# Gate and up units in four PSUM banks, four units written where the value weights were, and the last tile's column pieces one after the other

## The chip, the cores and the metric

The kernel runs on one core of one Trainium2 chip. The metric is the device time of one execution in microseconds (us). Before the change it is 226.32 us, the median of 3 runs (226.05 to 226.35).

## The reference, cut to what matters

For 2048 tokens of 512 features, with LayerNorm output xn shared by two branches:

```
xn  = layernorm(x)
q, k, v = heads(xn @ wqkv)                     # 32 heads of 16
phi(a)  = [softmax(a @ w_phi), softmax(-a @ w_phi)]
kv, z   = sum over tokens of phi(k) v^T, sum over tokens of phi(k)
A   = (phi(q) kv) / (phi(q) z + 1e-6) @ wo     # linear attention: kv needs all tokens
B   = ((xn @ w_gate) * (xn @ w_up)) @ w_down   # 1792 hidden features
out = x + A + B
```

All inputs and the output are bfloat16.

## The kernel before, in words

Tokens go in 16 tiles of 128 (index t) and in 4 groups of 512 (index g). The hidden features of branch B go in 14 blocks of 128 (index ft). The work falls into these pieces; each is a Python function that records steps for the engines:

- `ln`/`emit_xn` (lines 410 to 445): LayerNorm of a tile on VectorE, and its transpose, by TensorE for t below 8 and by a transposing DMA on SyncE's queue for the rest.
- `wprime(w)`: folds `w_phi` into the key weights (w=1) or the query weights (w=0); four steps of four small matmuls, each copied out by ScalarE.
- `k_pe(t)`: values of a tile, 4 matmuls of 512 columns that read the value weights `wv`, copied out by ScalarE. `k_pe(12)` to `k_pe(15)` are the last readers of `wv`.
- `k_pk(t)` and `k_norm(t)`: the keys' softmax. `emit_exp` (line 463) has ScalarE copy the 512 columns twice (plain and negated), VectorE take a maximum by a tree (L476) and subtract it (L482), and ScalarE take the exponential. `emit_sums` (L496) is a tree of additions on VectorE; `k_norm` then takes a reciprocal (L520) and multiplies (L523).
- `emit_kv(half)`: the sum over 8 token tiles, 64 matmuls of 65 columns for each half. `emit_kv(1)` needs `k_norm(15)`, the last of the keys, and `q_pk` writes banks that it uses.
- `q_pk(t)`, `q_scale(t)`, `q_T(t)`, `q_num(t)`, `q_oT(t)`: the queries' softmax by the same trees, a transposing DMA of 128x1024 on SyncE's queue, 8 matmuls of 68 columns into banks 3 and 4, a division on VectorE (L614, L615), and a second transposing DMA.
- `glu(g, ft)`, a unit: 4 matmuls of 512 columns for the gate and 4 for the up projection, each into a PSUM bank of its own. ScalarE copies the gate bank to SBUF (L277, the line of every ScalarE step), and VectorE multiplies it with the up bank (L545) into the hidden buffer `hT`.
- `final(t)`: 18 matmuls for a tile's output (14 blocks of `w_down`, 4 of `wo`), in three steps of 7, 7 and 4; VectorE adds x (L642) and SyncE's queue stores the tile. The last tile is cut into columns 0 to 383 and 384 to 511, which lie in banks 7 and 5.

All matmuls are issued by one helper at L297.

PSUM has 8 banks. Up to the queries, `next_a` (line 430) hands out banks 0 to 4 in turn for transposes, `k_pe`, `k_pk`, `wprime` and `emit_kv`. The units rotate through banks 5, 6 and 7 while g is below 3: one unit has 5 and 6, the next 7 and 5, the next 6 and 7. Units of g=3 alternate gate in 5 and up in 6; in the queries' stage banks 0 to 2 belong to `q_pk`, 3 and 4 to `q_num`, and 7, 5, 6 to `final`.

The hidden buffer of g=2 and 3, `hTb`, lies where the normalized keys `ek` lie, so units of g=2 with their place in `hTb` and all of g=3 are bound to when `ek` has been read: those of g=2 go over the keys of tiles 0 to 6, which `emit_kv(0)` has read, those of g=3 over the keys of tiles 7 to 13, most of which `emit_kv(1)` reads.

The order of the steps on each engine is set at build time. A list scheduler, `_order` (line 714), walks through all steps with estimated costs; an engine takes the step that can start first by the estimate, and of those that can start the one of lowest priority number. Steps count in the order they are written; units have priorities from 1e6, `final` from 2e6, so they fill what the others leave. Copies and multiplies of the units have -1 and the output additions -2. On the chip each engine then runs its own steps strictly in that order and waits with semaphores, and SyncE's queue issues its DMAs in order as well. So a change of a bank or of a place changes which steps depend on which, and through the estimate the order on all engines.

Of the kernel before, what the change touches and what calls it, by code (L numbers as in the profile page):

```python
# [197 lines left out]
def _build(nc, es, A_x, A_wqkv, A_w_phi, A_wo, B_w_gate, B_w_up, B_w_down, out):  # L198
# [59 lines left out]
    def sbv(name, lo, n):  # L258
        off = layout[name] + lo
        return arena[:, off:off + n]  # L260
# [5 lines left out]
    def bank(b, lo=0, n=512):  # L266
        return psum[:, b * 512 + lo: b * 512 + lo + n]
# [4 lines left out]
    def act_op(out_ap, in_ap, func=ACTF.Copy, scale=1.0, bias=None, prio=None):  # L272
        def fn(e):
            kw = {}
            if bias is not None:
                kw["bias"] = bias
            return e.activation(out=out_ap, in_=in_ap, func=func, scale=scale, **kw)  # L277
        r = [in_ap]
        if isinstance(scale, bass.AP):
            r.append(scale)  # L280
        if isinstance(bias, bass.AP):
            r.append(bias)
        return sc.step(ACT, fn, reads=r, writes=[out_ap], cost=(50.0 if str(in_ap.tensor.name) == "ps" else 95.0) + 0.833 * in_ap.free_size(),
                       lat=180.0, prio=prio)

    def dve(fn, reads, writes, n, rate=1.0, fixed=65.0, prio=None):
        return sc.step(DVE, fn, reads=reads, writes=writes, cost=fixed + rate * n / 0.96, lat=150.0, prio=prio)
# [4 lines left out]
    def mms(items, prio=None, warm=False):  # L292

        def fn(e):
            ins = None
            for o, l, r, a, z in items:
                ins = e.matmul(o, lhsT=l, rhs=r, start=a, stop=z)  # L297
            return ins
        reads = []
        writes = []  # L300
        c = 0.0
        for o, l, r, a, z in items:
            reads += [l, r]
            writes.append(o)
            c += max(25.0, o.free_size() / 2.4 + 2.3) * (1.6 if warm else 1.0)
        return sc.step(PE, fn, reads=reads, writes=writes, cost=c, lat=260.0, prio=prio)

    def group(o, pairs):
        n = len(pairs)
        return [(o, l, r, i == 0, i == n - 1) for i, (l, r) in enumerate(pairs)]  # L310
# [8 lines left out]
    def x_tile(t):  # L319
        return sbv("x", t * 512, 512)  # L320
# [3 lines left out]
    def xnT(q, s_lo, n):  # L324
        return sbv("xnT", q * S_TOK + s_lo, n)
# [17 lines left out]
    def load_wT(w, at):  # L343

        return sc.dma(SP, wT_v[:, w, :, :], A_wqkv[:, w * 512:(w + 1) * 512], transpose=True, at=at, issue=4600.0)
# [80 lines left out]
        return sbv("xn", (t % 4) * 512, 512)  # L426

    a_bank = [0]

    def next_a():  # L430
        b = a_bank[0] % 5
        a_bank[0] += 1
        return b

# [15 lines left out]
    def wprime(w):  # L450
        for dt in range(NQ):
            b = next_a()
            mms([(bank(b, jt * 128, 128), wT_v[:, w, jt, dt * 128:(dt + 1) * 128], wbd_v[:, jt, :], True, True)
                 for jt in range(NQ)])
            act_op(Wp_v[:, w, dt, :], bank(b))
# [50 lines left out]
    def k_pe(t):  # L506
        b = next_a()
        mms(group(bank(b), [(xnT(q, t * 128, 128), wv_v[:, q, :]) for q in range(NQ)]))
        act_op(vext_all[:, t, :, 0:64], bank(b).rearrange("p (c j) -> p c j", c=8))

    def k_pk(t):
        b = next_a()
        mms(group(bank(b), [(xnT(q, t * 128, 128), Wp_v[:, 1, q, :]) for q in range(NQ)]))
        p_slot["k", t] = emit_exp(b, ek_v[:, t, :])

    def k_norm(t):
        slot = t % 3
        sm = emit_sums(ek_v[:, t, :], p_slot["k", t], slot)
        rs = rs_v[:, slot, :]
        dve(lambda e: e.reciprocal(out=rs, in_=sm), [sm], [rs], 64, rate=6.0)  # L520
        e4 = ek_v[:, t, :].rearrange("p (g f h) -> p g f h", g=16, f=16)
        r4 = rs.rearrange("p (g h) -> p g h", g=16)
        dve(lambda e: e.tensor_tensor(out=e4, in0=e4, in1=r4[:, :, None, :].to_broadcast([128, 16, 16, 4]),  # L523
                                      op=ALU.mult), [ek_v[:, t, :], rs], [ek_v[:, t, :]], 1024, rate=0.5)


    def hT(g, ft, lo, n):
        return sbv("hTa" if g < 2 else "hTb", ((g % 2) * NF + ft) * 512 + lo, n)

    glu_ctr = [0]  # L530

    def glu(g, ft, banks):
        i = glu_ctr[0]
        glu_ctr[0] += 1
        bg = banks[(2 * i) % len(banks)]
        bu = banks[(2 * i + 1) % len(banks)]
        gr = sbv("gring", (i % 3) * 512, 512)
        base = 1e6 + i * 10
        mms(group(bank(bg), [(wg_v[:, q, ft * 128:(ft + 1) * 128], xnT(q, g * 512, 512)) for q in range(NQ)]),
            prio=base)  # L540
        mms(group(bank(bu), [(wu_v[:, q, ft * 128:(ft + 1) * 128], xnT(q, g * 512, 512)) for q in range(NQ)]),
            prio=base + 1)
        act_op(gr, bank(bg), prio=-1.0)
        dst = hT(g, ft, 0, 512)
        dve(lambda e: e.tensor_tensor(out=dst, in0=bank(bu), in1=gr, op=ALU.mult), [bank(bu), gr], [dst], 512,  # L545
            prio=-1.0)
# [5 lines left out]
    def emit_kv(half):  # L552
        for g in range(8):
            b = next_a()
            mms(group(bank(b, 0, 65), [(ek_v[:, t, g * 128:(g + 1) * 128], vext_all[:, t, g, 0:65])
                                       for t in range(half * 8, half * 8 + 8)]))
            kp = kvp_v[:, g, :]
            if half == 0:
                act_op(kp, bank(b, 0, 65))
                continue  # L560
            dve(lambda e, b=b, kp=kp: e.tensor_tensor(out=kp, in0=bank(b, 0, 65), in1=kp, op=ALU.add),  # L561
                [bank(b, 0, 65), kp], [kp], 65)
            dve(lambda e, kp=kp, g=g: e.tensor_tensor(
                out=kvx_v[:, g, 0:64].rearrange("p (h d) -> p h d", h=4),
                in0=kp[:, 0:64].rearrange("p (h d) -> p h d", h=4),
                in1=maskh[:, :, None].to_broadcast([128, 4, 16]), op=ALU.mult),
                [kp, maskh], [kvx_v[:, g, 0:64]], 64)
            dve(lambda e, kp=kp, g=g: e.scalar_tensor_tensor(
                out=kvx_v[:, g, 64:68], in0=maskh, scalar=kp[:, 64:65], in1=eps4, op0=ALU.mult, op1=ALU.add),
                [kp, maskh, eps4], [kvx_v[:, g, 64:68]], 4)  # L570
# [56 lines left out]

    def final(t, b, cols=(0, 512)):
        g, lo = t // 4, (t % 4) * 128
        base = 2e6 + t * 10  # L630
        c0, c1 = cols
        ob = bank(b, c0, c1 - c0)
        items = [(hT(g, ft, lo, 128), wd_v[:, ft, c0:c1]) for ft in range(NF)]
        items += [(oT_v[:, q, t * 128:(t + 1) * 128], wo_v[:, q, c0:c1]) for q in range(NQ)]
        items = group(ob, items)
        for k in (0, 7, 14):
            mms(items[k:k + 7], prio=base)
        i = out_ctr[0]
        out_ctr[0] += c1 == 512
        og = sbv("ostg", (i % 2) * 512 + c0, c1 - c0)  # L640
        xs = x_tile(t)[:, c0:c1]
        dve(lambda e: e.tensor_tensor(out=og, in0=ob, in1=xs, op=ALU.add), [ob, xs], [og], c1 - c0, prio=-2.0)  # L642
        sc.dma(SP, out_flat[t * 128:(t + 1) * 128, c0:c1], og, is_out=True)


    units = [(g, ft) for g in range(NG) for ft in range(NF)]

    def some_glu(n, g_max):
        for _ in range(n):
            if units and units[0][0] <= g_max:  # L650
                glu(*units.pop(0), (5, 6, 7) if units and units[0][0] < 3 else (5, 6))

    def ln(t0, n):
        emit_ln_stats(t0, n)
        for t in range(t0, t0 + n):
            emit_xn(t)
# [7 lines left out]
    make_wbd()  # L664
    wprime(1)
    for b0 in range(0, NT, 4):
        if b0 < 12:
            ln(b0 + 4, 4)
        if b0 == 8:
            load_wT(0, 0.0).deps.append(sc.by_eng[SP][-2])  # L670
            emit_kv(0)
            some_glu(99, 2)
        for t in range(b0, b0 + 4):
            k_pk(t)
            k_norm(t)
            if b0 < 8:
                some_glu(2, 1)
        if b0 < 12:
            for t in range(b0 + 4, b0 + 8):
                k_pe(t)  # L680
        if b0 == 8:
            wprime(0)
    emit_kv(1)
    some_glu(99, 3)
    LEAD = 2
    for t in range(NT + LEAD + 1):
# [9 lines left out]
    for t in range(NT - 1):  # L696
        final(t, 7 if t < 4 else (7, 5, 6)[t % 3])
    final(NT - 1, 7, (0, 384))
    final(NT - 1, 5, (384, 512))

# [151 lines left out]
```

## Time and profile before

| What | Value |
|---|---|
| median of 3 runs | 226.32 us |
| the profiled execution, its own time | 225.87 us |
| its span, first to last instruction | 224.1 us |
| VectorE (DVE) busy | 192.2 us, 86% |
| ScalarE (ACT) busy | 115.4 us, 51% |
| granted TensorE clock, mean | 1.0 |
| bytes read and written in HBM | 8.67 MB and 2.10 MB |

In the profile PE is TensorE's matmuls, PEld its weight loads, DVE VectorE, ACT ScalarE, POOL GpSimd and SP SyncE, with "q" for an engine's sequencer or queue. `L297` is line 297. `arena` is the one SBUF tensor, so tiles are told apart by line and by order; `ps` is PSUM. Matmuls overlap one another in the trace (a 512-column matmul has a row of about 0.38 us, yet the next starts 0.216 us after it), so their rate is read from start to start.

### The profile page before, as it was taken

The numbers are of one execution on the slowest core, as the hardware profiler recorded it, in microseconds if no ns is written. First come the engines' busy times: TensorE is split into PE (matmuls) and PEld (weight loads), VectorE is DVE, ScalarE is ACT, GpSimd is POOL, SyncE is SP. The second block draws the span as 40 slices with busy tenths as digits, with TensorE's granted clock in tenths as the row PEclk, the third lists the DMA queues.
The fourth block names the chain that finished last, engine by engine and source line by source line (L and its number), as shares of the span: only waits on it lengthen the run. The fifth ranks groups of instructions, "written<-read, shape, count | busy, mean of one in ns | idle before, by whom it ended". The sixth has DMA issues, their size and how long they took to land.

```text
span 224.1 us, 3616 instructions
## 1 busy us (share of the span) xinstructions
PE 218.5 (97%) x1312; PEld 106.3 (47%) x1312; DVE 192.2 (86%) x552; ACT 115.4 (51%) x193; POOL 9.6 (4%) x25
## 2 busy tenths in 40 slices
PE   8999999999999999998999999989999999999994
PEld 8455444444455444433364454444544444454443
DVE  5959999999982999999989999989999999974121
ACT  2669977673526997654529766636443343100000
POOL 4252000000030000000000000000000000000000
PEclk9999999999999999999999999999999999999999
DMA  6999921300014400000000143543465643673201
GB/s 174 331 319 397 352 72 28 70 0 0 0 24 74 97 0 0 0 0 3 0 1 3 31 86 70 87 81 70 94 73 109 135 108 77 138 146 70 68 23 48
DMA packets 44210, 19.39 MB, mean 87 GB/s; under 512 B 35232, under 2 KB 43168, under 8 KB 44192
## 3 DMA queue, kind: packets, MB, share of 16 engines
q1 hardware_dynamic: 44192, 19.16, 35.1%
q8 instruction: 10, 0.16, 0.3%
q14 instruction: 8, 0.07, 0.1%
HBM read 8.67 MB, written 2.10 MB: 48 GB/s over the span
## 4 chain that ended last, share of the span: by engine, by line
PE 81%; DVE 13%; DMA 2%; ACT 1%; issue 1%; DVEq 0%
PE ps L297 81%; DVE arena L496 3%; DVE arena L545 3%; DVE arena L476 2%; DMA arena<-arena 2%; DVE arena L482 2%; ACT arena L277 1%; DVE arena L615 1%; DVE arena L601 0%; DVE arena L598 0%; DVE arena L614 0%; DVE arena L523 0%; DVE arena L642 0%; DVE arena L599 0%; DVEq L194 0%
## 5 line engine op out<-in xcount | busy, mean ns | idle before, releaser
L297 PE MATMUL ps<-arena 128*128 128x512 bf16 (+4 forms) x1312 | 218.5, 330 | 2.8 <-DVE arena L368 1.0
L297 PEld LDWEIGHTS ps<-arena 128*128 128x128 bf16 x1312 | 106.3, 99 | 114.9 <-ACT arena L277 7.6
L277 ACT ACTIVATE arena<-ps 128x512 bf16<-128x512 f32 (+1 forms) x160 | 84.5, 605 | 48.0 <-PE ps L297 43.0
L277 ACT ACTIVATE arena<-arena 128x1024 bf16<-128x1024 bf16 x32 | 34.5, 1081 | 30.4 <-DVE arena L482 29.4
L496 DVE TENSOR_TENSOR arena<-arena 128x512 f32<-128x512 bf16 (+3 forms) x128 | 49.2, 395 | 0.1
L545 DVE TENSOR_TENSOR arena<-ps,arena 128x512 bf16<-128x512 f32 x56 | 37.8, 677 | 2.4 <-PE ps L297 1.4
L476 DVE TENSOR_TENSOR arena<-arena 128x256 bf16<-128x256 bf16 (+3 forms) x128 | 31.4, 271 | 2.6 <-ACT arena L277 2.5
L642 DVE TENSOR_TENSOR arena<-ps,arena 128x512 bf16<-128x512 f32 (+2 forms) x17 | 11.0, 652 | 12.7 <-PE ps L297 12.5
L482 DVE TENSOR_TENSOR arena<-arena 128x1024 bf16<-128x1024 bf16 x32 | 21.6, 675 | 0.0
L413 DVE BATCH_NORM_STATS2 arena<-arena 128x6 f32<-128x512 bf16 x16 | 10.6, 683 | 2.2 <-DMA arena<-in_A_x_dram 2.2
L523 DVE TENSOR_TENSOR arena<-arena 128x1024 bf16<-128x1024 bf16 x16 | 10.9, 680 | 0.0
L615 DVE TENSOR_TENSOR arena<-ps,arena 128x512 bf16<-128x512 f32 x16 | 10.7, 671 | 0.1
L614 DVE RECIPROCAL arena<-ps 128x32 f32<-128x32 f32 x16 | 5.4, 341 | 4.5 <-PE ps L297 4.4
L520 DVE RECIPROCAL arena<-arena 128x64 bf16<-128x64 f32 x16 | 8.7, 542 | 0.1
L436 DVE TENSOR_SCALAR arena<-arena 128x512 bf16<-128x512 bf16 x16 | 6.2, 407 | 2.2 <-issue 1.5
L601 DVE TENSOR_TENSOR arena<-arena 128x512 bf16<-128x512 bf16 x16 | 6.6, 410 | 0.0
L422 POOL TENSOR_TENSOR arena<-arena 128x1 f32<-128x1 f32 (+1 forms) x7 | 5.3, 764 | 4.1 <-DVE arena L420 3.9
L598 DVE RECIPROCAL arena<-arena 128x32 f32<-128x32 f32 x16 | 5.4, 335 | 0.0
L420 POOL TENSOR_SCALAR arena<-arena 128x4 f32<-128x4 f32 x3 | 1.1, 380 | 50.5 <-DVE arena L415 50.5
L599 DVE TENSOR_TENSOR arena<-arena 128x32 bf16<-128x32 f32 x16 | 2.8, 172 | 0.0
L561 DVE TENSOR_TENSOR arena<-ps,arena 128x65 f32<-128x65 f32 x8 | 1.4, 216 | 0.8 <-PE ps L297 0.8
L415 DVE BATCH_NORM_AGGREGATE arena<-arena 128x2 f32<-128x6 f32 x16 | 1.9, 159 | 0.1
(19 smaller groups left out, 9.7 us busy)
## 6 DMA issues: line engine op xcount, KB each, us to landing
out_dram<-arena SPq DMA_DIRECT2D x15, 128.0 KB, 1.9
arena<-in_B_w_down_dram SPq DMA_DIRECT2D x1, 1792.0 KB, 17.1
arena<-in_B_w_gate_dram SPq DMA_DIRECT2D x1, 1280.0 KB, 8.6
arena<-in_B_w_up_dram SPq DMA_DIRECT2D x1, 1280.0 KB, 12.5
arena<-in_A_x_dram SPq DMA_DIRECT2D x1, 1024.0 KB, 5.9
arena<-arena SPq DMA_TRANSPOSE x40, 2.8
arena<-in_A_wqkv_dram SPq DMA_DIRECT2D x1, 512.0 KB, 4.3
arena<-in_A_x_dram SPq DMA_DIRECT2D x1, 512.0 KB, 5.3
```

What stands on the lines that cost most here:

```text
L277: return e.activation(out=out_ap, in_=in_ap, func=func, scale=scale, **kw)
L297: ins = e.matmul(o, lhsT=l, rhs=r, start=a, stop=z)
L413: dve(lambda e, t=t: e.bn_stats(stats_v[:, t, 0:6], x_tile(t)), [x_tile(t)], [stats_v[:, t, 0:6]], 512)
L476: dve(lambda e, dst=dst, src=src, k=k: e.tensor_tensor(out=dst, in0=src[:, :, 0:k], in1=src[:, :, k:2 * k], op=ALU.max), [src], [dst], 16 ...
L482: dve(lambda e: e.tensor_tensor(out=p4, in0=p4, in1=src[:, :, None, :].to_broadcast([128, 16, 16, 4]), op=ALU.subtract), [pst, src], [pst] ...
L496: dve(lambda e, dst=dst, src=src, k=k: e.tensor_tensor(out=dst, in0=src[:, :, 0:k], in1=src[:, :, k:2 * k], op=ALU.add), [src[:, :, 0:2 * ...
L520: dve(lambda e: e.reciprocal(out=rs, in_=sm), [sm], [rs], 64, rate=6.0)
L523: dve(lambda e: e.tensor_tensor(out=e4, in0=e4, in1=r4[:, :, None, :].to_broadcast([128, 16, 16, 4]), op=ALU.mult), [ek_v[:, t, :], rs], [ ...
L545: dve(lambda e: e.tensor_tensor(out=dst, in0=bank(bu), in1=gr, op=ALU.mult), [bank(bu), gr], [dst], 512, prio=-1.0)
L601: dve(lambda e: e.tensor_tensor(out=e1, in0=e1, in1=rs[:, :, None, :].to_broadcast([128, 8, 16, 4]), op=ALU.mult), [e1, rs], [e1], 512, ra ...
L615: dve(lambda e: e.tensor_tensor(out=o.rearrange("p (g h d) -> p g h d", g=8, h=4), in0=nd[:, :, 0:64].rearrange("p g (h d) -> p g h d", h= ...
L642: dve(lambda e: e.tensor_tensor(out=og, in0=ob, in1=xs, op=ALU.add), [ob, xs], [og], c1 - c0, prio=-2.0)
```

## The change

Three edits and what they need:

```diff
     a_bank = [0]
+    a_banks = [5]
     def next_a():
-        b = a_bank[0] % 5
+        b = a_bank[0] % a_banks[0]
...
     def hT(g, ft, lo, n):
+        if g == 3 and ft < 4:
+            return sbv("wv", ft * 512 + lo, n)
         return sbv("hTa" if g < 2 else "hTb", ((g % 2) * NF + ft) * 512 + lo, n)
...
     def final(t, b, cols=(0, 512)):
         g, lo = t // 4, (t % 4) * 128
-        base = 2e6 + t * 10
         c0, c1 = cols
+        base = 2e6 + t * 10 + (c0 > 0)
...
+    glu_banks = [(5, 6, 7)]
     def some_glu(n, g_max):
         for _ in range(n):
             if units and units[0][0] <= g_max:
-                glu(*units.pop(0), (5, 6, 7) if units and units[0][0] < 3 else (5, 6))
+                glu(*units.pop(0), glu_banks[0])
...
     for b0 in range(0, NT, 4):
+        if b0 == 4:
+            a_banks[0] = 4
+            glu_banks[0] = (4, 5, 6, 7)
...
         if b0 == 8:
+            some_glu(4, 3)
             wprime(0)
     emit_kv(1)
+    glu_banks[0] = (5, 6)
     some_glu(99, 3)
```

1. **Four banks.** From the second quarter of the tokens on, `next_a` hands out banks 0 to 3 only, and the units have banks 4 to 7: one unit 4 and 5, the next 6 and 7, so that gate and up each come back to a bank after two units. From the units behind `emit_kv(1)` on they have 5 and 6 as before.
2. **Four units of g=3 elsewhere.** The hidden blocks 0 to 3 of the last 512 tokens are written over `wv` and no longer over the keys, and the units are recorded before `emit_kv(1)`. They depend on the last `k_pe`, and no longer on `emit_kv(1)`.
3. **The last tile.** The piece of 128 columns has a priority number one higher than the piece of 384, so that it is not taken in turn with it.

The matmuls, copies, multiplies and DMAs are the same in number and size; no value is computed differently.

## The prediction

> **What bounds the kernel now.** First the page's head and busy shares, then who PE waited for, then the stage from 78 us to 112.5 us, then the chain that ended last, around its two joints off PE and at its end.
>
> ```profile
> span 224.1 us, 3616 instructions
> ...
> PE 218.5 (97%) x1312; PEld 106.3 (47%) x1312; DVE 192.2 (86%) x552; ACT 115.4 (51%) x193; POOL 9.6 (4%) x25
> ```
> ```profile
> PE ps L297 <- DVE arena L368: 1.0, 1, 1.0
> PE ps L297 <- ACT arena L277: 1.0, 2, 0.8
> PE ps L297 <- DMA arena<-arena: 0.7, 1, 0.7
> ```
>
> PE is the bound, and its named waits (us, times, longest) are few. Its busy time can hide short waits, so I read the trace from matmul start to matmul start. Undisturbed, 512 columns take 0.216 us, 384 take 0.162, 128 take 0.056, 65 or 68 take 0.030; the 1312 matmuls sum to 214.2 us. Above that the trace has 4.34 us up to 77 us (1.03 before the first matmul, the rest in the first 10 us), and 2.62 us from there to the end. These 2.62 are the most that better overlap can save inside: 0.11 at 87.3, 0.04 at 92.6, **0.94 at 103.0**, 0.08 at 111.7, 0.04 at 116.1 (together 1.21), then 0.20 at 135.4, **0.83 at 145.4**, 0.14 at 168.0 (together 1.17), and 0.24 in crumbs.
>
> ```profile
> 78.00:112.50 34.50, 33.72 (x162) 14.28 (x161) 34.32 (x88) 22.57 (x38) 0.00 (x0) 1.00 0.00 0
> ```
> ```profile
> 101.91 0.61 DVE arena L482
> 102.52 0.02 issue
> 102.54 1.55 ACT arena L277 x2
> 104.09 0.05 issue
> 104.14 1.90 PE ps L297 x8
> ```
>
> The columns of the first are the stretch, its length, then busy (count) of PE, PEld, DVE, ACT, POOL, the clock and DMA. In this stage VectorE has work all the time. The second is the chain (start, length): a subtraction in VectorE's queue, behind it ScalarE's exponential, and behind that a unit's gate copy that PE needed for its bank. The whole chain's later part:
>
> ```profile
> 141.57 4.82 DMA arena<-arena
> 146.39 0.05 issue
> 146.43 74.69 PE ps L297 x448
> 221.13 0.02 issue
> 221.15 0.56 DVE arena L642
> 221.71 0.20 DVEq L194
> ```
>
> `q_T(3)` took 4.82 us from issue to landing, and `q_num(3)` stood at the head of PE's queue for it. Then PE runs to its last matmul at 221.34. The last lines are the two additions, one behind the other.
>
> **How I carry rows over.** For both programs I have the static order on each engine. A step's arrival after the change is the sum of the distances above over PE's new order, plus 4.34 us and what I add as waits. For VectorE I sum the trace's row of each operation, less the 0.08 us by which neighbours overlap, from where its work begins. Slack is arrival less the end of what the step waits for.
>
> **Four banks, units' side (takes 1.21).** A unit's gate bank was copied out and needed again, like its up bank, within two half-units (2 x 0.86 us) of its last matmul; with four banks it is three. From `glu(2,0)` to `glu(3,0)`, in the sums, the least slack to a multiply is 0.71 us (`glu(2,3)`) and most are 1.2 to 1.5; to a gate copy the least is 1.0 (`glu(2,10)`, behind the exponential of `k_pk(14)`). So the five waits go: -1.21. If VectorE ran 0.7 us later than summed, the first would be back.
>
> **Four banks, other side (adds 0.2).** The ring of `next_a` loses a bank. Up to 72 us the least slack stays 0.3 (`k_pk(8)`, after the copy of `emit_kv(4)`). At 78 us ScalarE is backed up (the row of `k_pe(13)`'s copy ends at 78.33). The second step of `wprime(0)` now wants that bank and arrives at 78.18, with the matmuls of every later step behind it on PE: 0.2 us with the semaphore. Bounds: 0, if PE is that late anyway, and 0.8, with one more copy (0.60) ahead. The next ones have 0.3, 0.5 and 0.7.
>
> **Units over `wv`.** The order shows less than the words say: ahead of `emit_kv(1)` stand all of `glu(2,13)` and only the gate of `glu(3,0)`, in place of 7 matmuls of `final(0)`; its up matmuls stand within `emit_kv(1)`. PE has 5 matmuls more (1.08) before it and arrives at 113.5 as before (4.54 + 109.04 = 113.6). VectorE has one multiply more (0.60) ahead of `k_norm(15)`, which ended at 112.56 and by the sum ends at 112.9: no wait, 0.6 us spare. Cost and gain 0 by itself; its worth is that this cover stands when 1.21 us are gone. Without it PE would arrive 0.9 us sooner and wait 0.3.
>
> **The queries' stage (takes 1.17, gives 0.5 back).** `q_pk(0)` goes 1.94 us of matmuls later, so at 116.3 against 115.44, and VectorE's query work begins at 118.5 against 117.62. It has two multiplies (1.2) less to do up to `q_scale(15)`. With typical landings (3.0 to 3.3 us from issue) the slacks of `q_num(2)` to `q_num(15)` are 0.5 to 2.5, least at `q_num(5)`; `q_pk(7)` to `q_pk(14)` have 0.3 or more; the units' alternation 5, 6 has 0.3 or more. The waits at 135.4 and 168.0 go. What stays is the slow landing. Two of 16 `q_T` took over 3.5 us: number 3 (4.82) and number 7 (4.34). The DMA records show why those: a 16 KB packet of the instruction queue started at 144.19 and one at 165.48, and packets under way then took 0.9 to 1.6 us where others take 0.02. Such packets come every 114 to 133 matmuls, so with PE's position: after the change at 143.0 and 163.5. `q_T(3)` is issued at 142.0 and `q_T(7)` at 162.9, so both are met again. With 4.82, `q_num(3)` would wait 0.8; with a typical landing nothing. `q_num(7)` likewise. I take 0.3 and 0.2; bounds 0 and 1.6.
>
> The Trainium skill, "Runtime: NRT & Kernel Launch", section "Instruction fetch mechanics", says that crossing a 16 KiB boundary costs one mostly hidden step. By it this term is 0 and the time 223.7; the two landings above speak against it. It also has "Perfetto Trace Analysis", "Identifying the Most-Contended Engine": occupancy is a fair measure for VectorE, and the most occupied engine is to be improved first. By it the banks do nothing where VectorE has 34.32 of 34.50 us, and the time is 225.4; against it speaks that in this stage PE waited 0.78 us while VectorE's result that PE needs was 0.95 us early.
>
> **The last tile (takes 0.45).** Before, the 384-column addition starts at 221.15, 0.2 before PE's end, the other follows to 221.91, and the second store is issued at 222.13, lands at 223.66, and 0.44 later the span ends. After, the 18 narrow matmuls (18 x 0.056 = 1.0 us) run behind the wide ones; the wide addition (0.56) and its store's issue (0.33) lie beside them. The narrow addition starts 0.02 behind PE's end E and takes 0.28: store at E + 0.33 where it was E + 0.79. Bounds 0.2 (it takes the wide one's 0.56) and 0.57. The wide piece now wants `q_oT(15)` 0.8 us earlier, 10 us after its landing.
>
> **Sum.** -1.21 + 0.2 - 1.17 + 0.5 - 0.45 = -2.13 us. The profiled execution, 225.87 (span 224.1 and 1.8 around it), becomes 223.7. It lay 0.45 below the median of 226.32; from the median, 224.2 us.
>
> **Rivals.**
> 1. *Forecast*, 223.6 to 224.8: chance 0.55.
> 2. *The slow landings cost as much as before*: both `q_T` met for their whole 1.5 us, waits 1.6 for 0.5. 225.3. For it, the two packets' places; against it, that only some of the packets were held (15 at 145.0). 0.20.
> 3. *VectorE becomes the bound before `emit_kv(1)`*: it has no idle time there, so what PE gains it waits for at `k_norm(15)`; 1.21 given back, 225.4. Against it the 0.6 spare. 0.10.
> 4. *No slow landing*: term 0, 223.7 or lower to 223.4. 0.09.
> 5. *Slower*: VectorE's 78 us of query work, which begins 0.9 us later by the clock, runs slower per operation because ScalarE's and PE's turns in PSUM now fall otherwise, and every `q_num` waits. It decides from the point where the lateness passes the slack (0.5 to 0.9) and the 2.1 saved: 3.5% of 78 us is 2.7. Then 226.4, and 227.2 at 4.5%. The rows of L545 (0.677 us) show no such spread. 0.06.
>
> The change not doing what it says is settled for units over `wv` (half a unit for four), and costed so.
>
> **Numbers.** A run can tell 0.2% (0.45 us) from no change. Faster by more, below 225.87: 1 to 4 nearly whole, 0.91. Within: 0.04. Slower: 0.05. Range 223.4 to 225.4: it takes in the bounds of the landings, and leaves out 5 and the joint worst of 2 and 3.
>
> **What would show it.** PE from start to start: no distance above 0.35 us between 87 and 117, one of 0.2 near 78; `emit_kv(1)` begun at 113.4 to 113.8; `q_T(3)` and `q_T(7)`'s landings and the wait behind each; two stores 1 us apart at the end, and the end 2.3 us after PE's last matmul where it was 2.76. Waits between 87 and 113, or a `k_norm(15)` after 113.5, would make it wrong.

## The result and the profile after

The changed kernel takes **223.05 us** (median of 6 runs, 222.79 to 224.5), the kernel before in the same runs 226.28 us (226.05 to 226.44): the ratio is 0.9866, with a 95% interval of 0.984 to 0.9891. It gained 3.2 us where 2.1 were forecast, and lies 0.35 us below the range. The direction was right; the size was too small. One execution of a later run, the profiled one of E1, had a granted clock of 0.66 and took 329.98 us; it is left out of the times and the landings below.

The profiled execution of the changed kernel took 222.97 us. Its page begins, to be held against the head and busy shares of before:

```profile
span 221.2 us, 3597 instructions
...
PE 215.5 (97%) x1288; PEld 107.1 (48%) x1312; DVE 191.8 (87%) x552; ACT 116.1 (52%) x193; POOL 9.1 (4%) x25
```

There are 1288 matmuls for 1312 weight loads: the trace has lost 24 matmul records, mostly one after every 49 that are there. Each leaves a distance of 0.43 us between two starts where 0.216 belongs. These 24 gaps look like waits and are none (the weight loads are complete there), so I take 0.2155 us off for each; the same holds for the other traces that show fewer matmuls than loads. The view of who PE waited for (us, times, longest) now has the start alone:

```profile
PE ps L297 <- DVE arena L368: 1.0, 1, 1.0
PE ps L297 <- DVE arena L420: 0.7, 1, 0.7
PE ps L297 <- DVE arena L437: 0.4, 1, 0.4
```

L368, L420 and L437 are the first memset and the first LayerNorm, all within 10 us. The waits for ScalarE (L277) and for a transposing DMA (`arena<-arena`) are gone. The stretch from 78 to 112.5 us, with the same columns as in the prediction:

```profile
78.00:112.50 34.50, 34.29 (x166) 15.93 (x169) 34.20 (x86) 23.20 (x39) 0.00 (x0) 1.00 0.00 0
```

PE has 34.29 us where it had 33.72, although this trace misses some of its records, and VectorE is as full as before (34.20 against 34.32). The chain that ended last closes with one short addition behind PE, not two:

```profile
210.56 8.42 PE ps L297 x56
219.01 0.29 DVE arena L645
```

From start to start of the matmuls, the two profiled executions differ so:

| Part of the profiled execution | before | after | difference |
|---|---|---|---|
| lost in the first 10 us | 3.26 | 3.34 | +0.08 |
| waits over 0.03 us, 80 to 117 us | 1.21 | 0 | -1.21 |
| waits over 0.03 us, 117 us to PE's end | 1.16 | 0 | -1.16 |
| crumbs behind 10 us | 0.29 | 0.22 | -0.07 |
| PE's last matmul to the span's end | 2.80 | 2.28 | -0.52 |

The sum is -2.88 us; the span went from 224.14 to 221.25, -2.89.

### The profile page after: what moved, and what is told of

Read it like the earlier page. It is cut to its first block, busy times and chain, and to the rows that moved or that the text cites. A ratio compares the mean times of both kernels' runs of the same rounds, so it can differ in the third digit from the quotient of the medians.

```text
span 221.2 us, 3597 instructions
## 1 busy us (share of the span) xinstructions
PE 215.5 (97%) x1288; PEld 107.1 (48%) x1312; DVE 191.8 (87%) x552; ACT 116.1 (52%) x193; POOL 9.1 (4%) x25
## 4 chain that ended last, share of the span: by engine, by line
PE 73%; DVE 16%; SPq 4%; DMA 3%; issue 2%
PE ps L297 73%; DVE arena L548 4%; DVE arena L497 3%; DMA arena<-in_A_x_dram 3%; SPq L164 3%; DVE arena L477 3%; SPq L165 2%; DVE arena L413 2%; DVE arena L483 2%; DVE arena L521 1%; DVE arena L524 1%; DVE arena L437 0%; DVE arena L645 0%; DVE arena L415 0%
## 5 line engine op out<-in xcount | busy, mean ns | idle before, releaser
L297 PE MATMUL ps<-arena 128*128 128x512 bf16 (+4 forms) x1288 | 215.5, 328 | 3.5 <-DVE arena L368 1.0
L277 ACT ACTIVATE arena<-ps 128x512 bf16<-128x512 f32 (+1 forms) x160 | 84.6, 596 | 47.3 <-PE ps L297 44.1
L277 ACT ACTIVATE arena<-arena 128x1024 bf16<-128x1024 bf16 x32 | 34.1, 1069 | 29.3 <-DVE arena L483 28.8
L497 DVE TENSOR_TENSOR arena<-arena 128x256 f32<-128x256 f32 (+3 forms) x128 | 48.8, 392 | 0.1
L477 DVE TENSOR_TENSOR arena<-arena 128x256 bf16<-128x256 bf16 (+3 forms) x128 | 30.6, 267 | 2.9 <-ACT arena L277 2.8
L437 DVE TENSOR_SCALAR arena<-arena 128x512 bf16<-128x512 bf16 x16 | 6.1, 404 | 1.5 <-issue 1.5
L420 POOL TENSOR_SCALAR arena<-arena 128x4 f32<-128x4 f32 x3 | 0.7, 227 | 50.3 <-DVE arena L415 50.3
L571 DVE SCALAR_TENSOR_TENSOR arena<-arena 128x4 bf16<-128x4 bf16 x8 | 1.7, 218 | 0.0
```

Source lines behind the costliest of these rows:

```text
L477: dve(lambda e, dst=dst, src=src, k=k: e.tensor_tensor(out=dst, in0=src[:, :, 0:k], in1=src[:, :, k:2 * k], op=ALU.max), [src], [dst], 16 ...
L497: dve(lambda e, dst=dst, src=src, k=k: e.tensor_tensor(out=dst, in0=src[:, :, 0:k], in1=src[:, :, k:2 * k], op=ALU.add), [src[:, :, 0:2 * ...
```

## The experiments

Two questions were put to the chip. Which edit carries the gain: the four banks, or the units over `wv` that fill PE's time ahead of `emit_kv(1)`? And what were the landings of `q_T` worth, half of the waits? Theory A says that the banks take the waits away and that an instruction packet meeting a `q_T` is an accident of its own. Theory B says that VectorE bounds the stage, so that without the units over `wv` the banks bring nothing. All times are medians but that of E5, a single execution; the kernel before ran at 226.14 to 226.23 us beside them.

### One edit at a time: E1, E2, E3

```diff
 # E1: after, without the units over wv and the last tile's order
-        if g == 3 and ft < 4:
-            return sbv("wv", ft * 512 + lo, n)
...
-            some_glu(4, 3)
...
-        base = 2e6 + t * 10 + (c0 > 0)
+        base = 2e6 + t * 10
 # E2: after, without the banks and the last tile's order
-            a_banks[0] = 4
-            glu_banks[0] = (4, 5, 6, 7)
...
-        base = 2e6 + t * 10 + (c0 > 0)
+        base = 2e6 + t * 10
 # E3: before, with the last tile's order alone
-        base = 2e6 + t * 10
+        base = 2e6 + t * 10 + (c0 > 0)
```

> The kernel before with the first edit alone: banks 0 to 3 for next_a, 4 to 7 for the units, as in the change; the units of g=3 stay behind emit_kv(1) and the last tile's pieces are taken in turn. Theory A, that the waits that the four banks take from PE are the gain: PE's five distances above 0.216 us between 87 and 117 us are gone (1.21 us less), PE comes to emit_kv(1) about 0.9 us earlier than VectorE's k_norm(15) allows and waits about 0.3 there: 0.9 us less, and between 0 and 1.2 more of the queries' stage, as q_T(3) meets an instruction packet or not: 224.2 to 225.4 us. Theory B, that VectorE bounds the stage and the units over wv make the gain possible: PE waits for k_norm(15) what it gained, 226.0 to 226.4 us.

> The kernel before with the second edit alone: hidden blocks 0 to 3 of the last group over wv and their units recorded before emit_kv(1), with three banks 5, 6, 7. Theory A: the waits between 87 and 117 us stay, as they are of the banks; nothing but the queries' stage can move, by the place of an instruction packet against q_T(3): 226.3 us, at least 225.3. Theory B: the gain before emit_kv(1) appears here, about 1.2 us: 225.1 us, with the waits between 87 and 117 us gone.

> The kernel before with the third edit alone: the last tile's piece of 128 columns behind the one of 384. Both theories: 0.53 us less by the end of the trace of after, so 225.75 us; PE's waits as in before. If the waits move, it is the place of an instruction packet, since the order ahead of the last tile is the same; then the edits' effects do not add.

Measured: E1 (banks) **226.39 us**, ratio 1.0011 [0.9997, 1.0025], no gain at all. E2 (units over `wv`) **225.86**, 0.9993 [0.9981, 1.0005]. E3 (last tile) **225.5**, 0.9973 [0.9964, 0.9983], that is 0.6 to 0.7 us; its `q_T(3)` met a packet as before (4.62 us, a wait of 0.63).

E1 looks like theory B. E2 looks like neither: its waits in the profile are the old one for ScalarE at 102.8 us (0.92, as theory A wants) and a new one, of 1.12 us from start to start, behind a `q_T`. The first two lines are its view of who PE waited for, the others its chain:

```profile
PE ps L297 <- DMA arena<-arena: 1.0, 1, 1.0
PE ps L297 <- ACT arena L277: 0.8, 1, 0.8
```
```profile
161.47 4.74 DMA arena<-arena
166.21 0.05 issue
166.26 54.53 PE ps L297 x328
```

`q_T(7)` took 4.74 us; an instruction packet started at 163.91.

### Banks and units together: E4

```diff
 # after, without the last tile's order
-        base = 2e6 + t * 10 + (c0 > 0)
+        base = 2e6 + t * 10
```

> The change without its third edit: four banks and the units over wv, the last tile's pieces in turn. Theory A: after plus 0.53: 223.6 us, with no wait of PE behind the first 10 us. Against the run with the banks alone it tells what the units over wv are worth: 0.3 us by theory A (the wait at k_norm(15)), the whole gain before emit_kv(1) by theory B.

Measured: **223.66 us**, 0.9893 [0.9879, 0.9907], as expected (223.6). The trace has all its matmuls, and behind 10 us one distance of 0.26 too much, at 31.8 us, and no other above 0.03. So the effects do not add: banks alone +0.2 and units alone -0.3, together -2.5. Either the two need each other (theory B), or something unrelated hides what each is worth.

### Where the banks' gain went: E5

The kernel of E1 once more, unchanged, for a trace to read.

> The kernel with the four banks alone once more, for a trace at full clock: its twelve times of 225.6 to 227.2 us showed no gain, and theory A had 224.2 to 225.4. Theory B (VectorE bounds the stage ahead of emit_kv(1) without the units over wv): PE waits 1.2 us or more for k_norm(15) before emit_kv(1), and the waits at 87 to 103 us are gone. Theory A with an accident of landing (an instruction packet of 16 KB meets a q_T): the wait at k_norm(15) is about 0.3, and one or two waits of 0.8 to 1.2 us stand behind slow landings of q_T, over 4 us from issue, with an instruction packet inside.

Measured: 226.68 us. From 80 to 117 us PE has no wait, not even the 0.3 at `k_norm(15)`. What stands there instead is in the queries' stage, in the view of the waits and in the chain (start, length):

```profile
PE ps L297 <- DMA arena<-arena: 2.5, 2, 1.5
```
```profile
161.94 4.80 DMA arena<-arena
166.79 1.72 PE ps L297 x14
...
182.94 5.71 DMA arena<-arena
188.69 7.81 PE ps L297 x49
```

`q_T(7)` and `q_T(11)` landed after 4.80 and 5.71 us, with instruction packets of 16 KB started at 164.74 and 185.65 (and beside the second one of 8 KB, of another instruction queue, at 185.67), and PE waited 1.19 and 1.44 us for them (1.65 with the gap of a lost record in it). So the banks' 1.2 us were there, and 2.6 us went to two landings. Theory B is left with one way out: that these landings are a result of leaving the units out, and no accident.

### Moving the instruction packets: E6, E7, E8, E10

The packets of 16 KB come by PE's position in its instructions. To move them, I rewrote the warm-up ahead of the first transpose: the same columns in fewer, wider matmuls (or more, narrower ones). The order on every engine stays, behind the warm-up; the first 10 us are not quite the same.

```diff
 # E6 on before, E7 on the kernel of E2: 30 and 8; E8 on after: 12 and 17; E10 on after: 20 and 13
-    dve(lambda e: e.memset(zero, 0.0), [], [zero], 128)
-    mms([(bank(7, 0, 128), zero, zero, True, True)] * 46, warm=True)
+    wide0 = sbv("tree", 0, 256)
+    dve(lambda e: e.memset(wide0, 0.0), [], [wide0], 128)
+    mms([(bank(7, 0, 128), zero, zero, True, True)] * 30 + [(bank(7, 0, 256), zero, wide0, True, True)] * 8,
+        warm=True).cost = 46 * (128 / 2.4 + 2.3) * 1.6
```

> The kernel before with nothing but the warm-up ahead of the first transpose written differently: 30 matmuls of 128 columns and 8 of 256 in the place of 46 of 128, the same columns in 8 matmuls less, so that each instruction packet comes 8 matmuls later (about 1.7 us: 145.9 and 167.2 where it was 144.2 and 165.5). If the packet's meeting with q_T(3) made its landing slow: q_T(3) lands in 3.0 to 3.4 us, the wait of 0.83 at 145 us is gone, q_T(7) lands in at most 3.5 us, and the time is 225.4 us (226.2 less 0.83). If something else makes this landing slow, it stays at 4.8 us and the time at 226.2.

> The kernel with the units over wv alone and the same rewritten warm-up (8 matmuls less): packets at about 144.9 and 165.6 us, between the transposes, where 163.9 met q_T(7) and q_oT and made PE wait 1.12 us. If that wait was the packet's: it is gone, 224.8 us (225.9 less 1.1), so that the units over wv alone are worth about 0.6 us against the kernel before without its own meeting. Otherwise 225.9 us.

> The changed kernel with the warm-up in 17 matmuls less (12 of 128 columns and 17 of 256), so that a packet comes at about 144.0 us, within q_T(3)'s packets (143.2 to 145.2), where it came at 140.4. If the meeting makes the landing slow: q_T(3) lands over 4 us after its issue, PE waits 0.3 to 0.9 us for it, and the time is 223.4 to 223.9 us (223.05 and the wait). If the landing has nothing to do with the packet: 223.05 us and no wait.

> The changed kernel with the warm-up in 13 matmuls less (20 of 128 columns, 13 of 256). With 17 less the packet had come at 146.3 us, too late for q_T(3), no wait appeared, and 223.81 us came with about 0.5 more lost in the first 10 us. With 13 less it should start between 142 and 145 us, in or just ahead of q_T(3)'s packets (143 to 145.2). If it meets them: q_T(3) lands over 4 us after its issue, PE waits 0.3 to 0.9 us there, and the time is 224.1 to 224.7 us. If the meeting costs nothing or is missed: 223.1 to 223.8 us.

| Run | median us, ratio | packet and landing | wait of PE |
|---|---|---|---|
| E6 | **225.34**, 0.9964 [0.9939, 0.9988] | 145.65 and 167.48; `q_T(3)` 3.11, `q_T(7)` 3.24 | none for them |
| E7 | **224.79**, 0.9933 [0.9909, 0.9958] | 143.98 and 166.14; `q_T(7)` 3.25 | none for them |
| E8 | **223.81**, 0.9889 [0.985, 0.9929] | 146.26, too late; `q_T(3)` 3.24, `q_T(4)` 4.40 | 0.06 |
| E10 | **223.99**, 0.9903 [0.9889, 0.9918] | 144.72, within `q_T(3)`: 4.51 | 0.63 |

E6 and E7 came out at the expected 225.4 and 224.8: the waits at 145 us of the kernel before and at 165 us of E2 were the packets' meetings. In E6 the view of who PE waited for has no DMA any more:

```profile
PE ps L297 <- DVE arena L369: 1.1, 1, 1.1
PE ps L297 <- ACT arena L277: 0.8, 1, 0.8
PE ps L297 <- DVE arena L438: 0.7, 1, 0.7
PE ps L297 <- DVE arena L422: 0.5, 1, 0.5
```

Eight matmuls less in a warm-up are worth 0.8 us to the kernel before. So of the 3.2 us between before and after, some 0.8 are luck: the meeting that the changed kernel's packets happened to miss. Against E6 the changed kernel is 2.3 us faster (225.34 to 223.05).

E8 missed its aim: the packet moved by 5.9 us, not by 3.7, and met `q_T(4)`, which had the slack. Its 0.8 us over the changed kernel are not a meeting's; 0.4 us of them are in the profiled execution's first 10 us (3.76 against 3.34). E10 hit. The chain of its profiled execution (224.31 us) has it:

```profile
142.72 4.51 DMA arena<-arena
147.23 0.05 issue
147.27 73.05 PE ps L297 x444
```

The parts agree: 222.97, 0.65 more in the first 10 us (3.99) and the wait of 0.63 make 224.25. The median of E10, 223.99, is 0.1 below the band that I gave for a meeting, and only 0.2 above E8's: not every execution need meet alike, and only one of each has a trace. So the size of the effect is shown in the trace, and not in these two medians.

How a meeting looks is in the view of the DMA engines: 40 slices of each window, the first row their busy share in tenths, the second GB/s. First the changed kernel from 142 to 146.5 us, `q_T(3)` undisturbed:

```profile
DMA  1000100000289999999999469999510017994000
GB/s 11 9 9 9 16 0 0 0 0 0 36 175 212 223 218 214 209 203 209 193 173 205 82 143 218 212 221 205 123 21 0 0 46 246 337 373 155 9 0 0
```

Then E10 from 142.7 to 147.5 us, with the packet:

```profile
DMA  0000000000699999999996000000000999990299
GB/s 0 0 0 0 0 0 0 0 0 9 139 220 222 211 196 220 343 201 188 154 58 2 0 0 6 6 11 9 11 9 11 170 284 297 284 159 0 68 239 273
...
q8 instruction: 1, 0.02, 1.2%
```

Both move some 210 GB/s for `q_T(3)`'s bulk. With one 16 KB instruction packet in the window, the engines then stand at 0 to 11 GB/s for 10 slices, 1.2 us, before the rest comes. The DMA records have 20 packets of the transposes that were under way in it: they took 1.24 to 1.43 us each, where the median packet takes 0.02, and all ended within 0.04 us of each other, 0.8 us after the instruction packet.

### The banks alone, with the packets out of the way: E9, E11

```diff
 # E9 and E11: the kernel of E1; E9 has 34 of 128 and 6 of 256 columns (6 matmuls less), E11 14 more:
-    mms([(bank(7, 0, 128), zero, zero, True, True)] * 46, warm=True)
+    mms([(bank(7, 0, 128), zero, zero, True, True)] * 32 + [(bank(7, 0, 64), zero, zero[:, 0:64], True, True)] * 28,
+        warm=True).cost = 46 * (128 / 2.4 + 2.3) * 1.6
```

> The four banks alone with the warm-up in 6 matmuls less (34 of 128 columns, 6 of 256), so that the instruction packets that came at 164.7 and 185.7 us, within the transposes of q_T(7) and q_T(11), come about 1.5 us later, behind them. Theory A (the four banks' 1.2 us are real, and two landings met by packets gave back 2.85): no wait of PE behind 10 us, 223.6 to 224.2 us, as the change without its third edit (223.66), so that the units over wv are worth nothing by themselves. Theory B (the units over wv are what makes the banks pay): waits elsewhere take the place of these two, and the time stays above 225.5 us.

> The four banks alone with the warm-up in 14 matmuls more (32 of 128 columns, 28 of 64), so that the packets come some 3 us earlier than in the first run of the banks alone: 161.5 and 181.5 us in the place of 164.7 and 185.7, ahead of the packets of q_T(7) and q_T(11). With 6 less the packet had stayed within q_T(7)'s (165.1), PE waited 1.20 us, and q_T(11)'s wait of 1.65 was gone. Theory A: neither wait is there, 223.6 to 224.3 us (226.4 less 2.85, and up to 0.7 for q_T(14), which the last packet may meet). Theory B (without the units over wv waits of another kind hold the time): above 225 us.

Measured: E9 **225.11 us**, 0.9951 [0.9932, 0.997]; E11 **223.84 us**, 0.9886 [0.9866, 0.9906].

E9 is half of the test. The packet at 165.13 us was still within `q_T(7)` (4.81 us, a wait of 1.20), the other came at 188.86 and `q_T(11)` made no one wait (it still took 4.08 us, with a packet of 8 KB started at 186.09); the median fell by 1.3 us for the 1.44 that went. E11 is the whole: packets at 160.44 and 181.21, `q_T(7)` in 3.20 and `q_T(11)` in 3.96, and in the view of who PE waited for nothing later than the first tiles:

```profile
PE ps L297 <- DVE arena L368: 1.0, 1, 1.0
PE ps L297 <- ACT arena L277: 0.5, 1, 0.5
PE ps L297 <- DVE arena L438: 0.4, 1, 0.4
```

Its window at `q_T(7)`, 161.7 to 167 us, and below it that of E5, 161.9 to 167 us, the same kernel but for the warm-up:

```profile
DMA  0000000002999999999479997200000000000000
GB/s 0 0 0 0 0 0 0 0 0 39 213 216 222 209 209 209 199 195 199 88 145 209 218 213 157 32 0 0 0 0 0 0 0 0 0 0 0 0 0 0
```
```profile
DMA  0000000002999999999659999990000000010000
GB/s 0 0 0 0 0 0 0 0 0 38 205 217 213 211 219 199 205 187 195 135 79 219 345 209 203 67 4 0 0 2 8 10 10 8 10 18 0 0 0 0
...
q8 instruction: 1, 0.02, 1.2%
```

The bulk is the same in both. Without a packet the engines are done in slice 26; with it a trickle of 2 to 18 GB/s goes on up to slice 36, 1.2 us later.

Between E5's kernel (226.39 in E1) and E11's lie 2.55 us, and the traces put 2.63 us of waits behind two landings there. Theory B falls: with 223.84 the banks alone are within 0.2 us of banks and units together (223.66). Better overlap has little left to take from the changed kernel: behind the first 10 us its profiled execution has 0.22 us in crumbs, and no wait.

## Why the prediction was too small, step by step

- **Four banks, units' side (1.21): right.** The five waits are gone in every trace with four banks (E4, E5, E8 to E11). With three banks the large one stays: 0.92 in E2, E3, E6 and E7. The two small ones at 87 and 93 us are missing in all of these too, so they came and went between executions.
- **Four banks, other side ("adds 0.2"): failed.** The second step of `wprime(0)` began at 78.26, not 78.18, and `k_pe(13)`'s copy ended at 78.20, not 78.33. It waited 0.01. The step was a difference of two sums with 0.15 us between them, and the traces were off by 0.08 and 0.13.
- **Units over `wv` (0 by itself): right in size beside four banks, wrong in its reason.** Banks alone, packets aside, take as long as both within 0.2 us (E11, E4). With three banks the units are worth something: E7 lies 0.55 us below E6, whose trace has waits of 0.08 at 112 us and 0.20 at 136 us that E7's has not. So packets aside the two edits overlap in part, where the three medians had looked as if they needed each other. I wrote that without these units PE would reach `emit_kv(1)` 0.9 us sooner and wait 0.3. The order of E1 shows why it does not: with four banks the scheduler puts `glu(2,13)` and the gate of `glu(3,0)` ahead of `emit_kv(1)` in any case, 642 matmuls as with the units. The 0.6 us to spare at `k_norm(15)` were 0.25: it ended at 113.22 and `emit_kv(1)` began at 113.47, in the predicted window.
- **The queries' stage ("takes 1.17"): right. ("gives 0.5 back"): failed, and it is the largest part of the miss.** `q_T(3)` was issued at 142.02 us and `q_T(7)` at 162.84, as predicted (142.0, 162.9). But the packets that I had put at 143.0 and 163.5 came at 140.41 and 162.81, and both were over (at 141.71 and 163.77) before the bulk of the transposes moved (from 143.1 and 164.0). The landings were 3.23 and 3.04 us, the waits 0. Rival 4 had this case, at a chance of 0.09. The mechanism was right (E6, E10); its place was not to be had to within a `q_T`'s own 2 us. From the second on, packets came 114 to 135 weight loads apart in the traces of before and after, and 17 matmuls less moved one by 5.9 us in E8.
- **The last tile (0.45): right, 0.52 in the trace**, and 0.6 to 0.7 between the medians of E3 and before, and of E4 and the changed kernel.
- **The sum.** 223.74 was forecast for the profiled execution. Less 0.2, 0.5 and 0.07 for the tail, it is 222.97, as measured (0.08 more in the first 10 us and 0.07 less in crumbs cancel). The rest of the miss is the step from the profiled execution to the median: I added the 0.45 us by which before's lay under its median, and after's lay 0.08 under its own. Two things vary between executions of one order: the first 10 us (3.24 in E4, 3.26 before, 3.78 in E5, 4.11 in E3, all with the same warm-up) and the meetings (0.83 us before, 0.63 in E3). Before's profiled execution had one of the quickest starts. That after has less to lose to meetings, and so less offset, is argued, not shown.
- **The rivals.** 3 (VectorE as the bound) is out: VectorE is as full from 78 to 112.5 us as before (34.20 against 34.32), and yet PE waits for nothing there. The Trainium skill, "Perfetto Trace Analysis", section "Identifying the Most-Contended Engine", would have the most occupied engine improved first. Here VectorE was busy for 34.32 of 34.50 us before, nothing of its work was made cheaper, and one more bank for PE's results took PE's 1.2 us of waits away all the same. The other page, "Runtime: NRT & Kernel Launch", section "Instruction fetch mechanics", gave 223.7 us, from the median and with this term at 0: nearer than my 224.2. Yet its rule, that crossing a 16 KiB boundary is mostly hidden, held in the changed kernel by place alone: where a packet met a transpose with little slack, PE waited 0.63 to 1.44 us (E10, E2, E5).
- **The range** failed on its lower side. It ended at 223.4, the offset of 0.45 included in full, although I had the run of 226.05 beside the median of 226.32 as a sign that the offset is no constant.

## What to carry to other kernels

When an edit that should gain shows nothing, look first at what else stands in the trace: here 1.2 us of a real gain lay under two accidents of 2.6 us, and only moving the accident by itself (a warm-up in more or fewer instructions) told one from the other. Single-edit runs of a kernel whose timing meets something periodic do not add up; 226.39, 225.86 and 223.66 would have made a false story of two edits that need each other. And a term that depends on where a periodic event falls is better given as two cases than as a mean between them, and the offset from profile to median as a range.

## What the runs showed of the hardware

- **A transposing DMA that meets an instruction packet can be held up.** In the 12 traces other than E1's, 384 transposes were issued behind 120 us, with a median of 3.05 us from issue to landing. 25 took over 4.0 us, and 24 of those have a 16 KB packet of the instruction queue started between 0.3 us before their issue and 2.8 us after it; the other one (4.08 us, E9) has a packet of 8 KB there, of the second instruction queue (q14). The longest, 5.71, has both. Of the 311 transposes with neither in that time, the slowest took 3.61. Not each meeting is slow: 20 more transposes had a 16 KB packet in that time and landed in 2.39 to 3.99 us. Why the transposes' packets are held for so long is not shown.
- **A packet's place is not a count of matmuls alone.** The seventh packet started after 844 weight loads in the changed kernel and after 855 before, with as many matmuls in PE's program.
- **The matmul records have regular losses.** 24 of 1312 were missing in the traces of after and of E5, mostly one after every 49 recorded, and 23 or 24 in E6, E7, E8 and E11, while before, E2, E3, E4, E9 and E10 had all of them; the weight loads were complete in each.
